# Two raw weight tiles placed in the empty half of the w_in buffer, with a new pinned order that reaches into batch 3

## The chip, the cores and the metric

The kernel runs on one core of a Trainium2 chip. The metric is the device time of one execution in microseconds (us); below, a median of three runs. The profile is one further execution recorded by the hardware profiler. PE is TensorE (matmuls), PEld its weight loads, DVE is VectorE, ACT is ScalarE, POOL is GpSimd, SP is SyncE, whose queue (SPq) issues the DMAs.

## What is computed

Slot attention over 8 batches, 8 heads, 576 positions, head size 64 and 32 slots, then a feed-forward block with weights `w_in` (512 x 2048) and `w_out` (2048 x 512):

```
a    = softmax(phi, over positions)
k_m  = einsum('bhsm,bhsd->bhmd', a, k);   v_m = einsum('bhsm,bhsd->bhmd', a, v)
attn = softmax(q @ k_m^T / 8, over slots)
x    = (attn @ v_m) with heads side by side          # 4608 x 512
out  = gelu(x @ w_in) @ w_out                        # gelu with erf
```

`w_in` and `w_out` reach the chip as 64-bit numbers, so the kernel decodes them as well.

## The kernel before

**What is on the engines.** x is never formed. For each batch `u_p` multiplies the value slots into a block of w_in (tile `pu`, line 598) and stores it as two float32r parts in a tile `U` (`Uh`, `Ul`, line 814), so that the hidden layer `h` (line 855) is attention probabilities `p_hi`, `p_lo` times U. GELU runs on ACT (`gf`, lines 867 to 876). Its result is split into `gh` (a cast) and `gl` (line 882, DVE), and `project` (line 895) multiplies these with `wo_hi` and `wo_lo` into four accumulators `acc`, 12 matmuls a step. Batches 0 and 1 go in turn over the first 8 column blocks f of the 16 of w_in, then over the last 8; batches 2 to 7 follow one after the other.

**How a weight tile is decoded.** Each f has a 1 MB raw tile, half for w_in (`Lwi`) and half for w_out (`Lwo`), loaded in two DMAs by `load_w` (line 251). For each half ACT runs `dec_b` (lines 272 and 273), DVE runs `dec_c`, `dec_g`, `dec_s` (lines 277, 281, 285) and POOL adds the two parts (`dDi`, `dDo`, line 305). The w_in half goes to `w_in_sb[:, :, f*128 : f*128+128]`; the w_out half is split into `wo_hi` (`dE`, a cast) and `wo_lo` (`dF`, line 311). `w_in_sb` has four sections of 2048 columns for each partition; columns 1024 and on of each are first written by f = 8.

**What sets the order.** `START` is a list of pieces by name and number, a letter behind a colon choosing the engine (`d` DVE, `a` ACT). It is executed as written; what is left goes by due times (`put`, `run`). At the end each engine's instructions are chained to their program order, so every engine's queue, SP's too, runs strictly in that order. `HOME` names the buffer of each tile. Raw tiles share five buffers `U0` to `U4` of 32 KB a partition with the first key and value tiles and with the U tiles.

**The start.** Batch 0's chain is `phi`, its exponential, transposes `pt` with copies to `aT` (`atc`, line 210), slot sums `pk` for keys (line 531), `km`, `tn`, copy to `k_blocks`, scores `psc` in three parts (line 615), softmax (`n_max` line 634, `n_sub` and `n_mul` line 639, `n_exp` line 646, `n_sum` line 649), transposes `pT` (line 674), `p_hi` and `p_lo` (lines 689, 693), and the first `h`. Batch 1's transposes `pt` and its `pk` follow. `W` pieces are single warm-up matmuls. `anorm` makes the reciprocal sums `rz` that `km` needs. For batch 1 the PSUM tiles of `pt`, `pk`, `tn`, `pu` and `psc` share one buffer, so each waits for the copies of the one before.

Of the kernel before, what the change touches and what calls it, by code (L numbers as in the profile page):

```python
# [35 lines left out]
o_2_0:wy1 U_3_0:U4 U_3_1:U0 o_2_1:wy1 U_3_2:U2 U_3_3:U1 kv_6_0_0:kv5 kv_6_0_1:kv3 kv_6_0_2:kv4
kv_6_0_3:kv2 kvw_6:wy1 kv_6_1_0:kv0 kv_6_1_1:kv7 kv_6_1_2:kv6 kv_6_1_3:kv1 kv_7_0_0:kv5
kv_7_0_1:kv3 kv_7_0_2:kv4 kv_7_0_3:kv2 kvw_7:wy0 kv_7_1_0:kv0 kv_7_1_1:kv7 kv_7_1_2:kv6
kv_7_1_3:kv1 o_3_0:wy1 U_4_0:U3 U_4_1:U4 o_3_1:wy1 U_4_2:U0 to_3:wy1 U_4_3:U2 o_4_0:wy1 U_5_0:U1
U_5_1:U3 U_5_2:U4 U_5_3:U0 o_4_1:wy0 o_5_0:wy1 U_6_0:U2 U_6_1:U1 U_6_2:U3 o_5_1:wy0 U_6_3:U4  # L40
to_5:wy1 o_6_0:wy0 U_7_0:U0 U_7_1:U2 U_7_2:U1 U_7_3:U3 o_6_1:wy1 o_7_0:wy0 o_7_1:wy1 to_7:wy0
# [13 lines left out]
n_sub.2 dB.2.1 dG.2.1 dC.2.1 at.1.1.0 dS.2.1 n_hi.0 at.1.0.0 Lkv.1.0.4 n_lo.0 h.0.0.0
atc.1.1.0 Lkv.1.1.0 atc.1.0.0:d at.1.0.4 n_exp.2 n_sum.2 n_inv.2 n_mul.2 atc.1.0.4:d
dB.3.1 n_hi.1 dC.3.1 dDo.2 dG.3.1 dS.3.1 dDo.3 anorm.1 at.1.1.4 n_T.2 atc.1.1.4
gelu.0.0.0 n_hi.2 Lwi.3 slots.1.0 km.1.0 Lkv.1.1.1 n_lo.2 n_lo.1 h.0.0.1 dB.3.0 dC.3.0
dS.3.0 dE.2 Up.0.2.1 Lkv.1.1.2 gelu.0.0.1 Lwo.4 Uh.0.2 Lkv.1.1.3 h.0.1.0 gelu.0.1.0
h.0.1.1 dG.3.0 dF.2 Ul.0.2 gh.0.0:a gl.0.0 dB.4.1 dC.4.1 dG.4.1 Lkv.1.1.4 slots.1.1  # L60
h.0.2.0 dS.4.1 km.1.1 slotsT.1 kT.1:d Lwi.4 dDi.3 Lwi.5 Lq.1.0 gelu.0.1.1 gh.0.1:a
dB.4.0 h.0.2.1 Up.0.3.1 p.0.0 gl.0.1 dE.3 dG.4.0 dDo.4 dE.4 dF.4 gelu.0.2.1 Uh.0.3
Ul.0.3 score.1.0 dC.4.0 dS.4.0 Lwi.6 gelu.0.2.0 h.0.3.0 Lwo.7 gh.0.2:a dF.3 dB.5.0
gelu.0.3.0 h.0.3.1 dDi.4 dB.6.0 sT.1.0.1 Lwo.5 dB.5.1 sT.1.0.0 Lwi.8 Up.0.4.1 p.0.1
dC.5.0 dS.5.0 dG.5.0 Uh.0.4:d Ul.0.4 h.0.4.0 gelu.0.3.1 gh.0.3:a max.1.0 dG.6.0 Lq.1.1
dDi.5 Up.0.5.1 h.0.4.1 sub.1.0 exp.1.0 gl.0.2 dC.6.0 gl.0.3 dG.5.1 dC.5.1 dS.5.1 sum.1.0
gelu.0.4.1 p.0.2 Uh.0.5:d Ul.0.5 inv.1.0 dDo.5 dE.5 mul.1.0 dS.6.0 score.1.1 pT.1.0
Lwo.6 dB.6.1 Lwo.8 sT.1.1.0 p.0.3 sT.1.1.1 gelu.0.4.0 Lwi.7 gh.0.4:a dF.5 dB.7.1 gl.0.4
dG.6.1 dDi.6 Up.0.6.1 Uh.0.6 ph.1.0:d dC.7.1 h.0.5.0 h.0.5.1 dB.7.0 Ul.0.6 dC.6.1
max.1.1 dG.7.0 gelu.0.5.1 gelu.0.5.0 Up.1.0.4 Uh.1.0 dC.7.0 dS.7.0 sub.1.1 h.0.6.0  # L70
gelu.0.6.0 Lphi.2.1 dDi.7 amax.2.1 gh.0.5:a Ul.1.0 gl.0.5 pl.1.0 exp.1.1 dS.6.1 dDo.6
dE.6 h.0.6.1 gelu.0.6.1 p.0.4 Up.0.7.1 Uh.0.7:d sum.1.1 dS.7.1 inv.1.1 p.0.5 gh.0.6:a
# [24 lines left out]
h.0.14.0 dG.15.1 dDo.15 h.0.14.1 gelu.0.14.0 h.0.15.0 Lq.2.0 p.0.13 dE.14 gelu.0.14.1
h.0.15.1 mr.2 Lkv.2.0.4 dF.14 gelu.0.15.0 h.1.8.0 gelu.0.15.1 gh.0.14 gl.0.14 gh.0.15:a
dE.15 anat.2 p.0.14 h.1.8.1 gelu.1.8.1 gl.0.15 Lkv.2.1.0 dF.15 p.0.15 o.0.0.15
gelu.1.8.0 gh.1.8 o.0.1.15 o.0.2.15 o.0.3.15 h.1.9.0 h.1.9.1 gelu.1.9.1 anorm.2   # L100
gelu.1.9.0 gl.1.8 Up.1.12.4 h.1.10.0 gelu.1.10.0 Lkv.2.1.1 Lkv.2.1.4 gh.1.9:a gl.1.9 Lkv.2.1.2
Lkv.3.0.0 p.1.8 p.1.9 Uh.1.12 Lkv.2.1.3 Ul.1.12 slots.2.0 slots.2.1 h.1.10.1
gelu.1.10.1 km.2.0 km.2.1 slotsT.2 h.1.11.0 kT.2:d score.2.0 gelu.1.11.0 h.1.11.1 gelu.1.11.1
sT.2.0.1 sT.2.0.0 max.2.0 gh.1.10 Lkv.3.0.1 h.1.12.0 gl.1.10 Up.2.0.4 Uh.2.0 Ul.2.0 Lphi.3.0 gh.1.11
h.1.12.1 gelu.1.12.1 gelu.1.12.0 sub.2.0 p.1.10 h.1.13.0 Lq.2.1 gh.1.12:a gl.1.11
Lphin.3 p.1.11 Lkv.3.0.2 exp.2.0 sum.2.0 gl.1.12 inv.2.0 mul.2.0 pT.2.0 score.2.1
# [1118 lines left out]
```

## Time and profile before

| | us |
|---|---|
| median of 3 runs (702.25, 702.95, 704.43) | 702.95 |
| the profiled execution, device time | 704.61 |
| its span, first to last instruction | 702.8 |
| what lies around the span | 1.81 |
| PE busy in the span | 691.1 |
| DVE, ACT, POOL busy | 388.6, 298.4, 46.6 |
| mean granted TensorE clock | 0.981 |

The clock is given as a share of 2.4 GHz, so 0.50 is the lower level, 1.2 GHz. A window row gives, for each engine, the busy us and, in brackets, how many instructions. A timeline row gives the start, the duration and the instruction; `[idle ... <-releaser]` at its end is idle time before it and what ended that. Successive short instructions overlap a little, so durations add up to somewhat more than the stretch they fill.

### The profile page before, as it was taken

What the parts mean: (1) busy time and instruction counts of PE and PEld (TensorE: products, weight loads), DVE (VectorE), ACT (ScalarE), POOL (GpSimd) and SP (SyncE); (2) the same over time, 40 slices, a digit from 0 to 9 for tenths busy, and PEclk for the clock granted to TensorE, in tenths of its full rate; (3) what the DMA queues carried; (4) which work ended last, traced back from release to release, by engine and by line L of the source; (5) the groups of instructions that cost most, each with busy time, mean ns of one, the idle gap of its engine ahead of it and who ended that gap; (6) DMA issues with size and microseconds to landing.
All of it is one profiled execution on the core that took longest, in us unless ns stands there. A gap on an engine that the chain in (4) does not pass through costs nothing.

```text
span 702.8 us, 12357 instructions
## 1 busy us (share of the span) xinstructions
PE 691.1 (98%) x4940; PEld 576.6 (82%) x4940; DVE 388.6 (55%) x705; ACT 298.4 (42%) x768; POOL 46.6 (7%) x39
## 2 busy tenths in 40 slices
...
PEclk7599999999999999999999999999999999999999
...
GB/s 318 329 211 172 154 197 62 133 29 212 86 142 117 177 217 23 65 137 159 190 1 32 82 2 31 1 98 1 30 1 31 83 1 31 1 31 0 31 1 45
DMA packets 30716, 64.37 MB, mean 92 GB/s; under 512 B 3780, under 2 KB 8644, under 8 KB 30660
## 3 DMA queue, kind: packets, MB, share of 16 engines
...
q10 hardware_dynamic: 96, 0.13, 0.1%
q14 instruction: 17, 0.14, 0.1%
...
## 4 chain that ended last, share of the span: by engine, by line
PE 94%; DMA 1%; DVE 1%; SPq 0%; ACT 0%; issue 0%
PE acc L895 50%; PE h L855 29%; PE tacc L895 6%; PE pu L598 4%; PE psc L598 1%; PE psc L506 1%; DMA raw<-w_in 1%; PE pk L531 1%; PE x L506 1%; SPq L345 0%; PE pk L506 0%; PE psc L519 0%; PE psc L560 0%; DVE aT L210 0%; PE x L519 0%
## 5 line engine op out<-in xcount | busy, mean ns | idle before, releaser
L855 PE MATMUL h<-p_hi,U 128*128 128x288 f32 x1024 | 203.8, 298 | 0.0
L895 PE MATMUL acc<-wo_hi,gh 128*128 128x512 f32 x512 | 200.6, 392 | 0.0
L895 PE MATMUL acc<-wo_hi,gl 128*128 128x512 f32 x512 | 199.7, 390 | 0.0
L895 PE MATMUL acc<-wo_lo,gh 128*128 128x512 f32 x512 | 199.6, 390 | 0.0
L867 ACT ACTIVATE gf<-h 128x256 f32<-128x256 f32 x192 | 74.0, 387 | 265.0 <-issue 206.4
L855 PEld LDWEIGHTS h<-p_hi,U 128*128 128x128 f32 x1024 | 164.0, 188 | 23.0 <-issue 8.3
L210 DVE CAST gh<-gf 128x512 fp32r<-128x512 f32 x109 | 46.9, 430 | 167.4 <-ACT gf L867 165.3
L895 PEld LDWEIGHTS acc<-wo_hi,gh 128*128 128x128 f32 x512 | 96.5, 188 | 21.1 <-DVE gl L882 3.4
L895 PEld LDWEIGHTS acc<-wo_hi,gl 128*128 128x128 f32 x512 | 96.1, 188 | 21.5 <-DVE gl L882 0.9
L895 PEld LDWEIGHTS acc<-wo_lo,gh 128*128 128x128 f32 x512 | 96.1, 188 | 15.8
L855 PE MATMUL h<-p_lo,U 128*128 128x288 f32 x512 | 108.8, 294 | 0.1
L882 DVE TENSOR_TENSOR gl<-gf,gh 128x512 fp32r<-128x512 f32 x128 | 94.3, 736 | 15.2 <-ACT gh L210 5.7
L855 PEld LDWEIGHTS h<-p_lo,U 128*128 128x128 f32 x512 | 81.4, 188 | 0.6 <-DVE p_lo L693 0.6
L814 DVE TENSOR_TENSOR U<-pu,U 128x512 fp32r<-128x512 f32 (+2 forms) x50 | 40.8, 834 | 42.0 <-ACT U L210 41.8
L869 ACT ACTIVATE tails<-h 128x32 f32<-128x32 f32 x192 | 37.4, 195 | 0.0
L598 PE MATMUL pu<-w_in_sb,kT 64*32 64x512 f32 (+2 forms) x624 | 34.4, 528 | 0.4 <-ACT kT L210 0.4
L210 ACT CAST U<-pu 128x512 fp32r<-128x512 f32 (+2 forms) x42 | 30.4, 759 | 7.4 <-PE pu L598 7.3
L305 POOL TENSOR_TENSOR w_in_sb<-y,raw 128x512 int32<-128x512 int32 x16 | 23.8, 1493 | 43.8 <-DVE y L285 11.8
L305 POOL TENSOR_TENSOR y<-y,raw 128x512 int32<-128x512 int32 x16 | 21.9, 1374 | 56.5 <-DVE y L285 23.9
L272 ACT ACTIVATE y<-raw 128x512 f32<-128x512 f32 x32 | 21.6, 675 | 8.9 <-issue 4.3
L895 PE MATMUL tacc<-wo_hi,gh_t 128*128 128x512 f32 x64 | 25.0, 391 | 0.0
L895 PE MATMUL tacc<-wo_hi,gl_t 128*128 128x512 f32 x64 | 24.9, 389 | 0.0
...
## 6 DMA issues: line engine op xcount, KB each, us to landing
...
raw<-w_out SPq DMA_DIRECT2D x16, 512.0 KB, 5.6
raw<-w_in SPq DMA_DIRECT2D x16, 512.0 KB, 4.5
out<-o SPq DMA_DIRECT2D x16, 512.0 KB, 2.7
...
aT<-phiN SPq DMA_DIRECT2D x6, 512.0 KB, 4.7
...
```

Source lines behind the costliest of these rows:

```text
L210: return e.copy(dst, src) if e is nc.scalar else e.tensor_copy(dst, src)
L272: nc.scalar.activation(y, high.bitcast(F32), AF.Abs, scale=2.0**16)
L305: nc.gpsimd.tensor_tensor(w, y, low, op=ALU.add)
L506: nc.tensor.matmul(pk[32 * j : 32 * j + 32, : 2 * D], st["aT", b][:, c, g, 32 * j : 32 * j + 32], st["kv", b, g, c][:, :, j, :], start=(c ...
L531: nc.tensor.matmul(pk[32 * j : 32 * j + 32, w0 * D : (w0 + n) * D], st["aT", b][:rows, c, g, 32 * j : 32 * j + 32], t[:rows, w0 : w0 + n, ...
L598: nc.tensor.matmul(ps[g][M * j : M * j + M], st["kT", b][rows, t, M * j : M * j + M], moving[j][rows], start=True, stop=True,)
L814: nc.vector.tensor_sub(u[:, ..., 1, :], pu, u[:, ..., 0, :].bitcast(F32))
L855: i = nc.tensor.matmul(h[:, :HS], u[g][w], x[:, g, :], start=(n == 0), stop=(n == 3 * G - 1))
L867: nc.scalar.activation(gf[:, f % 2 * n : f % 2 * n + n], h[:, :n], AF.Gelu)
L869: nc.scalar.activation(t, h[:, n:HS], AF.Gelu)
L882: nc.vector.tensor_tensor(g_of("gl", *k), g_of("gf", *k), g_of("gh", *k).bitcast(F32), op=ALU.subtract)
L895: nc.tensor.matmul(acc, x, w[:, f, :], start=(first and n == 0), stop=(last and n == 2))
```

## The change

Two raw tiles get another place: the raw tiles of f = 3 and f = 4 (`SPARE`) lie in columns 1024 and on of w_in_sb, sections 0 and 1 for f = 3, sections 2 and 3 for f = 4. `HOME` loses these two names and deals the five U buffers anew. `START` is a new list that goes on to loads, slots and scores of batches 4 to 6 and to hidden layers of batch 3. `PLACES` fixes at the start in what order tile tags get their memory. The output DMA of batches 0 and 1 is a piece of its own (`os`), so the list can put it later than the eviction. `anat` falls away, its halves `aadd` and `ax` being named apart.

```diff
 HOME = """
-raw_0:U0 ... raw_1:U2 ... raw_2:U1 ... raw_3:U0 ... raw_4:U2 ... raw_5:U3 raw_6:U1 raw_7:U0 ...
+raw_0:U0 ... raw_1:U2 ... raw_2:U1 ... raw_5:U0 raw_6:U2 raw_7:U1 ...
...
 START = """
-W.4.3 Lphi.0.0 amax.0.0 aexp.0.0 at.0.0.0 Lphi.0.1 amax.0.1 aexp.0.1 anorm.0 atc.0.0.0:d
...
+dG.1.1 atc.0.1.0 Lwi.0 dS.1.1 atc.0.0.4:a slots.0.0.0 dDo.1 Lphi.1.0 dE.1:d anorm.0 Lkv0.0.1 dF.1
...
+PLACES = """
+kT:1024*3 phi:4608*1 nm:8*2 sm:8*2 aT:5120*1 rz:8*2 ...
...
+    for x in PLACES.split():
+        tag, size, n = x.replace("*", ":").split(":")
+        sb.tile([P, int(size) // 4], F32, tag=tag, name=f"place_{tag}", bufs=int(n))
...
+    SPARE = {3: 0, 4: 2}
+
     def raw_of(f):
         def make():
-            if f == 0:
-                first_tiles()
+            if f in SPARE:
+                x = w_in_sb[:, SPARE[f] : SPARE[f] + 2, DFF // 2 :].bitcast(I32)
+                return x.rearrange("p k (n t) -> p k n t", t=2)
             return sb.tile([P, 2, DM, 2], I32, **home(f"raw_{f}"))
...
-        if f == NF - 1 and j % 2:
-            r = b * S + (j - 1) * P
...
+    def store(b, j):
+        r = b * S + (j - 1) * P
...
```

**DVE, from the maximum of the second score part of batch 0 (`mx_1`) to the product that ends its softmax (`s_1`, `smx_1`).** Tiles `y` and `raw` belong to the weight decode, `nm` to batch 1's phi. Before:

```order
L634 TENSOR_REDUCE mx_1_283<-psc_1_237 128x16
L639 TENSOR_TENSOR s_1_285<-psc_1_237,mx_1_283 128x512
L639 TENSOR_TENSOR s_0_231<-s_0_231,smx_0_249 128x512
L392 TENSOR_REDUCE nm_313<-phi_311 128x1
L649 TENSOR_REDUCE smx_1_315<-s_1_285 128x16
L653 TENSOR_SCALAR smx_1_315<-smx_1_315 128x16
L654 RECIPROCAL smx_1_315<-smx_1_315 128x16
L639 TENSOR_TENSOR s_1_285<-s_1_285,smx_1_315 128x512
```

In the changed order the last part of the same stretch, from the second sum on:

```order
L681 TENSOR_REDUCE smx_1_377<-s_1_357 128x16
L685 TENSOR_SCALAR smx_0_353<-smx_0_353 128x16
L686 RECIPROCAL smx_0_353<-smx_0_353 128x16
L313 TENSOR_SCALAR y_374<-y_374 128x512
L666 TENSOR_REDUCE mx_2_400<-psc_2_369 128x8
L671 TENSOR_TENSOR s_0_287<-s_0_287,smx_0_353 128x512
L685 TENSOR_SCALAR smx_1_377<-smx_1_377 128x16
L686 RECIPROCAL smx_1_377<-smx_1_377 128x16
L846 TENSOR_TENSOR U_0_399<-pu_0_390,U_0_399 128x2x128
L317 TENSOR_SCALAR w_in_sb<-w_in_sb 128x512
L671 TENSOR_TENSOR s_1_357<-s_1_357,smx_1_377 128x512
```

The first product (`s_0`) has moved behind the second sum, and a decode step, the third maximum, the first U and a decode step in the spare half stand ahead of the second product; the third score part on PE has moved ahead of the first `pu`.

**ACT, around the copies of batch 1's transposed phi (`aT<-pt`).** Before:

```order
L689 CAST p_hi_0_403<-pT_1_376 128x288
L210 COPY aT_396<-pt_0_397 128x4x128
L646 ACTIVATE s_2_390<-s_2_390 128x256
L272 ACTIVATE y_435<-raw_372 128x512
L273 ACTIVATE raw_372<-raw_372 128x512
L689 CAST p_hi_1_438<-pT_0_374 128x224
L689 CAST p_hi_1_438<-pT_1_376 128x224
L210 COPY aT_396<-pt_4_426 64x128
L873 ACT_TABLE_LOAD
```

And in the changed order:

```order
L721 CAST p_hi_0_443<-pT_1_410 128x288
L721 CAST p_hi_1_457<-pT_0_408 128x224
L721 CAST p_hi_1_457<-pT_1_410 128x224
L243 COPY aT_447<-pt_0_448 128x4x128 x2
L243 CAST wo_hi<-y_374 128x512
L243 COPY aT_447<-pt_4_480 64x128 x2
L721 CAST p_hi_1_457<-pT_2_489 128x64 x2
L905 ACT_TABLE_LOAD
```

All four copies are now on ACT; before, two of the four were on DVE.

**SP's queue, from the third raw tile to the loads behind batch 1's last key and value tiles (`kv_1_3`, `kv_1_4`), which wait for batch 1's first `pk`.** Before:

```order
L251 DMA raw_372<-w_in 128x1024
L345 DMA kv_1_1_483<-kv 128x512
L345 DMA kv_1_2_510<-kv 128x512
L251 DMA raw_515<-w_out 128x1024
L345 DMA kv_1_3_518<-kv 128x512
L345 DMA kv_1_4_548<-kv 64x512
L251 DMA raw_515<-w_in 128x1024
L251 DMA raw_587<-w_in 128x1024
```

And in the changed order (`w_in_sb` as a target is a raw tile in the spare half, f = 3 and then f = 4):

```order
L381 DMA kv_1_0_416<-kv 128x512
L287 DMA w_in_sb<-w_in 128x1024 x2
L357 DMA phi_486<-phiT 128x576
L381 DMA kv_1_4_518<-kv 64x512
L381 DMA kv_1_3_530<-kv 128x512
L287 DMA w_in_sb<-w_out 128x1024
L287 DMA raw_548<-w_out 128x1024
L287 DMA raw_554<-w_in 128x1024
```

The w_out half of f = 4 has moved behind the two waiting loads; the w_in halves of f = 3 and 4 and a load of batch 2's phi stand ahead of them.

## Rows read from the trace of the kernel before

**Rows 1.** The page: busy time, and granted clock in 40 slices.
```profile
PE 691.1 (98%) x4940; PEld 576.6 (82%) x4940; DVE 388.6 (55%) x705; ACT 298.4 (42%) x768; POOL 46.6 (7%) x39
...
PEclk7599999999999999999999999999999999999999
```

**Rows 2.** Windows by stage: PE, PEld, DVE, ACT, POOL busy, clock, DMA, GB/s.
```profile
15.07:25.40 10.33, 10.33 (x114) 9.38 (x114) 8.03 (x17) 3.56 (x7) 2.65 (x3) 0.50 1.03 380
...
34.00:35.74 1.74, 1.59 (x7) 0.78 (x6) 1.71 (x5) 1.73 (x4) 1.31 (x1) 0.97 0.74 298
35.74:37.51 1.77, 0.52 (x4) 0.28 (x3) 1.69 (x6) 1.07 (x5) 0.00 (x0) 1.00 0.02 9
37.51:40.90 3.39, 3.39 (x44) 2.53 (x45) 1.72 (x8) 2.63 (x6) 1.29 (x1) 0.50 0.34 117
40.90:47.33 6.43, 6.43 (x102) 5.12 (x101) 5.79 (x11) 6.25 (x16) 2.53 (x2) 1.00 1.00 358
...
60.00:120.00 60.00, 60.00 (x395) 48.62 (x394) 55.25 (x96) 42.09 (x91) 18.58 (x14) 1.00 0.37 130
120.00:360.00 240.00, 240.00 (x1876) 198.62 (x1876) 144.94 (x258) 114.67 (x271) 11.22 (x8) 1.00 0.41 124
```

**Rows 3.** Timeline of PE: start, duration, instruction, idle before.
```profile
15.07 7.06 PE L615 MATMUL psc<-k_blocks,q 128*128 128x64 f32 x32 [0.72 <-ACT k_blocks L210]
...
30.10 1.97 PE L674 MATMUL pT<-ident,s 128*128 128x128 f32 x8
31.98 1.94 PE L423 MATMUL pt<-ident,phi 128*128 128x128 f32 x8
33.57 0.76 PE L855 MATMUL h<-p_hi,U 128*128 128x288 f32 x2
...
37.51 2.52 PE L531 MATMUL pk<-kv,aT 128*32 128x128 f32 x40
...
43.59 1.43 PE L531 MATMUL pk<-kv,aT 128*32 128x128 f32 x40
...
47.33 0.50 PE L895 MATMUL acc<-wo_hi,gh 128*128 128x512 f32 x1
```

**Rows 4.** Timeline of DVE.
```profile
18.75 0.69 DVE L634 TENSOR_REDUCE mx<-psc 128x16 f32<-128x512 f32 x1 [0.67 <-PE psc L615]
...
27.66 0.69 DVE L639 TENSOR_TENSOR s<-s,smx 128x512 f32<-128x512 f32 x1
...
33.97 0.81 DVE L693 TENSOR_TENSOR p_lo<-pT,p_hi 128x288 fp32r<-128x288 f32 x2
34.70 0.68 DVE L210 COPY aT<-pt 128x512 f32<-128x512 f32 x1
...
43.81 1.10 DVE L882 TENSOR_TENSOR gl<-gf,gh 128x512 fp32r<-128x512 f32 x1 [0.29 <-ACT gh L210]
```

**Rows 5.** DVE groups by form: busy us, mean ns of one, idle before.
```profile
L281 DVE TENSOR_SCALAR raw<-raw 128x512 uint16<-128x512 uint16 x32 | 24.6, 789 | 0.1
...
L311 DVE TENSOR_TENSOR wo_lo<-y,wo_hi 128x512 fp32r<-128x512 f32 x16 | 13.2, 828 | 1.9 <-ACT wo_hi L210 1.8
```

**Rows 6.** Timeline of ACT.
```profile
34.02 0.58 ACT L210 COPY aT<-pt 128x512 f32<-128x512 f32 x1 [1.26 <-PE pt L423]
...
37.20 0.26 ACT L210 COPY aT<-pt 64x128 f32<-64x128 f32 x1 [0.69 <-PE pt L423]
```

**Rows 7.** Windows of 1 us, PE alone: busy, clock, DMA share, GB/s.
```profile
33.00:34.00 1.00, 1.00 (x7) 0.50 1.03 391
34.00:35.00 1.00, 0.85 (x4) 0.94 1.00 404
```

**Rows 8.** Timeline of SP's queue.
```profile
29.71 0.44 SPq L251 DMA_DIRECT2D raw<-w_out x1
38.23 0.90 SPq L345 DMA_DIRECT2D kv<-kv x2
```

**Rows 9.** The page's DMA issues: count, KB each, median us to landing.
```profile
raw<-w_out SPq DMA_DIRECT2D x16, 512.0 KB, 5.6
```

More of the change, by code (lines that the diff above doesn't have):

```diff
@@ L36 @@
[L36 to L41, printed above, removed]
+kv_1_0_0:kv6 y_2:wy0 U_0_0:U4 kv_1_0_1:kv1 kv_1_0_2:kv2 kv_1_0_3:kv5 kv_1_0_4:kv4 kv_1_1_0:kv3
@@ new lines @@
+kv_7_0_2:kv4 kv_7_0_3:kv2 kvw_7:wy0 kv_7_1_0:kv0 kv_7_1_1:kv7 kv_7_1_2:kv6 kv_7_1_3:kv1
+o_3_0:wy1 U_4_0:U4 U_4_1:U3 o_3_1:wy1 U_4_2:U2 to_3:wy1 U_4_3:U0 o_4_0:wy1 U_5_0:U1 U_5_1:U4
+U_5_2:U3 U_5_3:U2 o_4_1:wy0 o_5_0:wy1 U_6_0:U0 U_6_1:U1 U_6_2:U4 o_5_1:wy0 U_6_3:U3 to_5:wy1
+o_6_0:wy0 U_7_0:U2 U_7_1:U0 U_7_2:U1 U_7_3:U4 o_6_1:wy1 o_7_0:wy0 o_7_1:wy1 to_7:wy0
+"""
+PLACES = """
+kT:1024*3 phi:4608*1 nm:8*2 sm:8*2 aT:5120*1 rz:8*2 mx:72*2 smx:72*2 U0:8192*1 U4:8192*1
+kv0:2048*1 U3:8192*1 kv7:2048*1 U2:8192*1 q:4608*1 tails:8192*1 wy0:4096*1 km:1024*1
@@ L55 @@
[L55 to L72, printed above, removed]
@@ L97 @@
[L97 to L106, printed above, removed]
-h.1.13.1 gelu.1.13.0 p.1.12 ph.2.0:d Lkv.3.0.3 Lphi.3.1 h.1.14.0 sT.2.1.0 sT.2.1.1
-max.2.1 sub.2.1 gelu.1.13.1 gh.1.13 gl.1.13 h.1.14.1 exp.2.1 p.1.13 sum.2.1 pl.2.0
@@ new lines @@
+kT.1:d gelu.0.2.0 dC.4.0 Up.0.3.1 dC.4.1 dG.4.1 p.0.0 Uh.0.3 dE.3 dG.4.0 gh.0.1:a dS.4.1
+gelu.0.2.1 dS.4.0 dDo.4 Ul.0.3 dF.3 gh.0.2:a score.1.0 dDi.4 dE.4 h.0.3.0 sT.1.0.0 Lq.1.1
+dB.5.0 sT.1.0.1 Lwo.6 h.0.3.1 gl.0.1 dB.5.1 Up.0.4.1 dC.5.0 dG.5.0 p.0.1 Uh.0.4:a gelu.0.3.0
+dF.4 gelu.0.3.1 dC.5.1 dB.6.0 dS.5.0 gl.0.2 dDi.5 Ul.0.4 h.0.4.0 max.1.0 h.0.4.1 sub.1.0
+Up.0.5.1 dS.5.1 exp.1.0 dG.5.1 p.0.2 Uh.0.5:a sum.1.0 dDo.5 inv.1.0 Ul.0.5 gelu.0.4.0 dG.6.0
+Lwi.8 gelu.0.4.1 dB.6.1 Lwo.7 mul.1.0 h.0.5.0 dC.6.0 gh.0.3:a h.0.5.1 dS.6.0 dE.5 gl.0.3 dDi.6
@@ new lines @@
+score.1.1 gh.0.4:a pT.1.0 gelu.0.5.0 p.0.3 gelu.0.5.1 sT.1.1.1 amax.2.1 dC.6.1 mw.2 sT.1.1.0
+aexp.2.0 Lwo.8 gl.0.4 dG.6.1 Up.0.6.1 dF.5 p.0.4 Uh.0.6 aexp.2.1 dS.6.1 gh.0.5:d dB.7.0 dDo.6
+Ul.0.6 max.1.1 ph.1.0:a gl.0.5 Lwi.9 dB.7.1 Up.1.0.4 Lwo.9 dG.7.0 Lphin.2 dC.7.0 dE.6:a
+h.0.6.0 sub.1.1 Uh.1.0 dS.7.0 p.0.5 dC.7.1 dDi.7 exp.1.1 Ul.1.0 pl.1.0 gelu.0.6.0 dG.7.1
+Up.0.7.1 dS.7.1 h.0.6.1 Uh.0.7:a dDo.7 Ul.0.7 h.0.7.0 sum.1.1 gelu.0.6.1 inv.1.1 h.0.7.1
+gelu.0.7.0 dF.6 gh.0.6:a h.1.0.0 dE.7:a Lwi.10 gl.0.6 gelu.0.7.1 p.0.6 dF.7 dB.8.1 gh.0.7:d
@@ new lines @@
+Up.2.0.4 Lkv.3.0.0 Lq.2.1 gelu.1.12.0 h.1.13.0 os.0.1 Uh.2.0:d mw.4 h.1.13.1 gelu.1.13.0
+Lphi.5.1 Lkv.3.0.1 p.1.11 gelu.1.13.1 gh.1.12:a gl.1.12 sub.2.0 aadd.3 h.1.14.0 h.1.14.1
+gelu.1.14.0 gh.1.13:d h.1.15.0 gl.1.13 p.1.12 gelu.1.15.0 gelu.1.14.1 exp.2.0 p.1.13 gh.1.14:d
+sum.2.0 gl.1.14 inv.2.0 mul.2.0 h.1.15.1 Ul.2.0 p.1.14 gelu.1.15.1 pT.2.0 gh.1.15:a gl.1.15
+ax.3 tg.1.0 p.1.15 ph.2.0:d o.1.0.15 pl.2.0 o.1.2.15 score.2.1 h.2.0.0 sT.2.1.0 sT.2.1.1
+h.2.1.0 amax.5.0 o.1.3.15 tp.1.0 gelu.2.1.0 max.2.1 os.1.3 sub.2.1 tg.1.1 exp.2.1 Up.2.4.4
@@ new lines @@
+tg.1.2 tp.1.1 anorm.4 Uh.2.4:d o.1.1.15 os.1.1 tg.1.3 tp.1.2 Lkv.3.1.0 Lq.3.0 Ul.2.4 Lkv.3.1.3
+Lq.3.1 sum.2.1 mr.4 h.2.2.0 inv.2.1 Lkv.3.0.3 mul.2.1 Up.2.8.4 gelu.2.2.0 Lkv.3.1.2 gelu.2.0.0
+gh.2.0.0:d tp.1.3 pT.2.1 Lkv.4.1.4 gl.2.0.0 ph.2.1:a Lkv.4.0.4 h.2.3.0 Lkv.3.1.4 h.2.4.0
+gelu.2.3.0 to.1 h.2.5.0 P.2.0.0 gelu.2.5.0 gelu.2.4.0 Lkv.3.1.1 gh.2.0.1:a gl.2.0.1 Uh.2.8:d
+h.2.6.0 Ul.2.8 P.2.0.1 gelu.2.6.0 gh.2.0.2:a gl.2.0.2 h.2.7.0 P.2.0.2 gelu.2.7.0 gh.2.0.3:a
+gl.2.0.3 P.2.0.3 h.2.8.0 h.2.9.0 gelu.2.8.0 h.2.10.0 Up.2.12.4 gelu.2.10.0 gelu.2.9.0
@@ L987, in slot_attention_gelu_ffn @@
         "Lwi": lambda f: load_w(0, f), "Lwo": lambda f: load_w(1, f),
-        "Lphin": load_phin, "mw": a_out, "mr": a_back, "anat": a_nat, "aadd": a_add, "ax": a_x, "amax": a_max, "aexp": a_exp, "anorm": a_norm,
+        "Lphin": load_phin, "mw": a_out, "mr": a_back, "aadd": a_add, "ax": a_x, "amax": a_max, "aexp": a_exp, "anorm": a_norm,
         "at": a_T, "atc": a_Tc, "slots": slots, "km": slots_m,
@@ L1000, in slot_attention_gelu_ffn @@
     }
+    st.update({("far", "pu", b, f): 1 for b in range(3, B) for f in (4, 12)})
+    st.update({("far", "psc", b, 1): 1 for b in range(3, B)})
+    st.update({k: 1 for k in (("far", "xt", 3), ("far", "pu", 2, 12))})
     done = set()
@@ L1033, in prepare @@
         put(tn - 1, f"Lphin.{b}")
-        put(tn + 1, f"anat.{b}", *(f"aexp.{b}.{g}" for g in range(G)), f"anorm.{b}")
+        put(tn + 1, f"aadd.{b}", f"ax.{b}", *(f"aexp.{b}.{g}" for g in range(G)), f"anorm.{b}")
     prepare(2, T2, T2 + 5)
```

153 lines of the change are left out of this document (92 added, 61 removed).

## The prediction

> **What bounds the kernel now.** I read the page first: PE is busy for 691.1 of 702.8 us, and all of the granted clock's shortfall is in the first slices [rows 1]. The windows by stage show where the rest is. From 60 to 360 us PE is busy without a gap at the full clock, while DVE and ACT have room, DVE little of it up to 120 us (55.25 of 60) [rows 2]. So from the first `project` on, at 47.33 [rows 3], PE is the bound, and its work there is the same in both orders: the same matmuls, and by the order the same 88 changes between 32-row and full-size ones, each of which costs a fraction of a microsecond. The end of the kernel therefore moves by as much as the first `project` does, plus any wait that the new order makes later. The same six `h` and four `pu` stand ahead of it on PE in both orders, so 47.33 is a fair mark.
>
> Ahead of that mark the timeline of PE has two kinds of loss. The clock is at its lower level, 0.50, from the scores (15.07) to 34 us and again from 37.51 to 40.90 [rows 2, 7], and PE waits between 34.0 and 37.5: it is busy 1.59 of 1.74 and then 0.52 of 1.77 us [rows 2]. What it waits for there are the copies of batch 1's transposes; the last one on ACT starts at 37.20, and `pk` follows at 37.51 [rows 3, 6]. The clock falls right after that thin stretch. DVE is the engine behind most of this: from 18.75 on its timeline has no idle time up to the `p_lo` at 33.97 and the copy at 34.70 [rows 4].
>
> **The change part by part.** *Up to the first scores: nothing.* The new list no longer puts a warm-up matmul ahead of `tn`, but it puts `anorm` behind `dE.1` on DVE, and that cast waits for POOL; `km`, and with it `tn` and the scores, need `rz`. By the durations this gives about 15.0 for the first score matmul against 15.07 [rows 3]. Bounds: 0.6 earlier if `rz` is not last, 0.3 later if the weight half that the decode needs lands late. I take nothing.
>
> *DVE ahead of the transposes: later by 1.0.* In the old order 19 DVE instructions run from the first maximum at 18.75 to the product that starts at 27.66 and ends at 28.35 [rows 4]: 9.60 us, 0.505 each. The new order has 26 in that place: `dS.0.1`, `wo_lo.0`, the second maximum of batch 1's phi, `dC.2.1`, the third maximum, the first U and `dG.3.1` have come in. Seven at 0.505 are 3.5; two of them are dear, 0.79 and 0.83 [rows 5], so I take 3.6 (bounds 3.0 and 4.2). The second product then ends at 31.95. In the old order PE reached its eight `pT` transposes at 30.10, later than their data, and the next ones, `pt`, at 31.98 [rows 3]. In the new order the second half of `pT` (half of 1.97) runs from 31.95, and `pt` starts at about 32.95: 1.0 later. The first `h` comes at 34.5 instead of 33.57 [rows 3].
>
> *The copies: earlier by 1.7.* The old order needed from the start of `pt` at 31.98 to 37.51 for the copies and the small transposes [rows 3], 5.5 us, because two of four copies stood in DVE's full queue; the one at 34.70 waited for both `p_lo` [rows 4]. Now all four are on ACT, behind `p_hi`, which is done by then. `pt` 32.95 to 34.55, two copies of 0.58 [rows 6] to 35.6, the small transposes behind the first `h`, at 36.1 with the lower clock or 35.6 with the full one, 0.3 for them, two copies of 0.26 [rows 6]: `pk` starts between 36.4 and 36.9. DVE's third product, which the `pT` ahead of `pk` needs, is done at about 36.1 and could push this to 37.3. I take 36.8, 0.7 before the old 37.51; this is the net of the loss above and the gain here.
>
> *From `pk` to the mark.* The old order has no PE wait from 37.51 to 47.33 [rows 2]: 9.82 us, of which 3.39 at the lower clock. At the full clock the same work would take 9.82 - 1.70 = 8.1. So the mark comes at 36.8 + 8.1 = 44.9 if the clock stays up (2.4 earlier), or at 46.6 (0.7 earlier) if it falls for as long as before. In the new order PE is idle for about 0.5 to 1.0 us in the stretch ahead of `pk` where it idled 1.4 us, which speaks for a shorter fall or none; that it now also waits for half a microsecond ahead of the second half of `pT` speaks against it.
>
> *The two tiles in the spare half.* They let the w_in halves of f = 3 and 4 be issued ahead of the loads that wait for batch 1's `pk`; before, SP stood there from 30.15 to 38.23 [rows 8]. PE does not wait for weights in the old order, so this alone is worth nothing; what hides it is PE's own unbroken work from 37.51.
>
> *Behind the mark.* DVE is nearly full to 120 us [rows 2], so what it must do ahead of each `gl` matters. The old first `gl` ends at 44.91, 2.4 ahead of its use [rows 4]. Summing the new order by durations, the first `gl` ends near 43.1, 1.8 ahead of a mark at 44.9, and later ones keep that lead, because twelve casts `gh` go from DVE to ACT, which is busy 42 of 60 us [rows 2]. I take no new wait. The later output DMAs, `PLACES` and the split of `anat` cost nothing: PE does not wait in 120 to 360 [rows 2].
>
> **The sum.** Against the profiled execution's own 704.61: 703.9 with the clock's second fall, 702.2 without it. The median is 1.66 lower than that execution, as much as one such fall costs, so some of the timed runs may not have had it. I therefore count 0.7 and half of the 1.7, that is 1.55, against the median: **701.4**.
>
> **The rivals.** *The clock stays up from 34 us, and the fall was in the timed runs too.* Then the whole 2.4 is gained, 700.5, and 699.9 if the scores also start 0.6 earlier. For it: the shorter idle time. Against it: the 1.66 between the profiled run and the median.
>
> *The clock comes up later than before.* In the old trace it rose at 34 us, directly behind 16 transposes and with only 0.4 us of `h`: 0.50 in the window from 33, 0.94 in the next [rows 7]. In the new order the transposes are broken by DVE. If it comes up at 40.9 only, some 4.0 us from the first `h` on run at half speed, and the mark comes at 36.9 + 8.1 + 2.0 = 47.0: 0.3 gained, 702.6. The Trainium skill, TensorE: Matmul & The Clock Gate, section "Part 4: PE-mode transpose", says that transposes do not count as PE activity in the same way; by that rule the clock would wait for the `h` themselves, this rival's case. The rise behind 16 transposes speaks against it, though 0.4 us of `h` lay there too.
>
> *A weight load behind the wait on SP holds up ACT: slower.* The w_out half of f = 4 is now behind the two key and value loads that wait for `pk`, and its decode on ACT stands ahead of GELU of the third `h`, the cast of the fourth U and two `gh`; on DVE the other part of that U is behind it. Issued at about 38.5, it lands at 44.1 by the median 5.6 [rows 9]. Two ACT steps, GELU, the U cast and the DVE step take some 2.6, so U is there at 46.7; PE needs it at 44.9 + 2.8 + 0.65 = 48.35. It decides from a landing at 45.8 on; at 48 it costs 2.2 and, as PE then idles, the clock's 1.7 again: 705.3. The old order had the same load ahead of the wait, issued at 29.71 [rows 8].
>
> **How the numbers follow.** The forecast of about 701.4 has 0.40; the full gain (700.5 or less) 0.33; the late clock (702.6) 0.12; the late load or another wait of its kind in a list this long (705.3) 0.15. A measurement of this kernel can tell about 0.3%, 2.1 us, from no change: 700.84 and 705.06 are the borders. So faster 0.33, same 0.52, slower 0.15. The range goes from 699.4 (both gains, and the lower bound of the DVE stretch) to 704.6, which leaves out most of the slower case and a little below.
>
> **What would show it right or wrong.** In the changed profile: the first score matmul at 15.0; the second product of the softmax on DVE ending near 31.95 and `pt` at 32.95; `pk` between 36.4 and 37.3; the windows from 34 to 41 with a clock above the old ones; the first `project` at 45 to 46.6, and no PE idle behind it. A DVE stretch no longer than the old one, scores well ahead of 15, or a PE wait between 47 and 120 us would prove the prediction wrong.

## The result: slower by 1.2%, and the profile after

| | before | after |
|---|---|---|
| median, us (4 runs each, taken in turn) | 703.44 | 712.01 |
| lowest and highest | 702.25, 704.43 | 711.07, 712.67 |
| the profiled execution, its span | 704.61, 702.8 | 711.07, 709.3 |
| first `project` on PE in that execution (the mark) | 47.33 | 44.58 |
| device time less the mark | 657.28 | 666.49 |

The ratio is 1.0123 (95% interval 1.0105 to 1.0142). The forecast was 701.4 with a range up to 704.6, so the result lies far outside. The last line of the table splits it at once: the start came out shorter, as forecast, and 9.2 us were lost behind the mark, where the forecast took nothing.

The page of the changed kernel, the rows that answer to [rows 1]: PE has the same busy time, in a longer span.

```profile
PE 691.1 (97%) x4940; PEld 575.4 (81%) x4940; DVE 377.6 (53%) x686; ACT 306.8 (43%) x789; POOL 46.4 (7%) x39
...
PEclk8599999999999999999999999999999999999999
```

The windows by stage, in the columns of [rows 2]. The stretch from 35.74 to 40.90, where PE idled and then ran at 0.50, is now nearly full (1.48 of 1.77 and 3.28 of 3.39) and at 1.00. The stretch from 120 to 360 us, which was full, now lacks 5.85 us of PE.

```profile
35.74:37.51 1.77, 1.48 (x42) 0.97 (x41) 1.18 (x8) 1.75 (x5) 1.29 (x1) 1.00 0.42 118
37.51:40.90 3.39, 3.28 (x42) 2.72 (x42) 2.44 (x7) 3.07 (x9) 1.64 (x1) 1.00 0.79 270
...
120.00:360.00 240.00, 234.15 (x1806) 193.04 (x1812) 133.24 (x239) 113.61 (x267) 8.46 (x6) 0.99 0.40 120
```

The waits of PE from the mark to 345 us (waited for; us in total, times, longest): one wait holds most of it.

```profile
PE acc L927 <- DVE gh L243: 4.7, 1, 4.7
PE psc L538 <- DVE sT L744: 0.7, 1, 0.7
PE acc L927 <- ACT gh L243: 0.4, 1, 0.4
```

The chain of waits shows what stands ahead of it (start, us, instruction). The first four are work for batch 6's phi, of which batch 3's `project` needs nothing; `gh` and `acc` are batch 3's:

```profile
315.21 0.76 DVE nm L428
315.99 3.85 DMA row<-nm
319.90 6.34 DMA cols<-row
326.26 1.23 DVE aT L518
...
328.01 0.44 DVE gh L243
328.49 4.75 PE acc L927 x12
...
338.58 2.73 PE acc L927 x12
```

The maxima `nm` of a phi go to DRAM in one small DMA (`row`, the piece `mw`), come back spread over all partitions in a second (`cols`, `mr`), and DVE adds them (`aadd`). The timeline of DVE around it:

```profile
306.14 0.75 DVE L428 TENSOR_REDUCE nm<-phi 128x1 f32<-128x576 f32 x1
...
314.61 0.69 DVE L914 TENSOR_TENSOR gl<-gf,gh 128x512 fp32r<-128x512 f32 x1 [5.92 <-ACT gh L243]
...
326.26 1.23 DVE L518 TENSOR_TENSOR aT<-aT,cols 128x1024 f32<-128x1024 f32 x1 [7.97 <-DMA cols<-row]
...
328.01 0.43 DVE L243 CAST gh<-gf 128x512 fp32r<-128x512 f32 x1
```

The first maximum runs at 306.14. The second, `amax.6.1`, stands behind a `gl` that waits 5.92 us for ACT's cast, so it ends at 315.95. The two DMAs and the gaps around them take until 326.26. DVE stands for 7.97 us at the addition, and the cast `gh` that `project` needs is queued behind it. PE stands 4.7 us; then the clock falls. Windows of 2 us there, in the columns of [rows 2]:

```profile
324.00:326.00 2.00, 0.00 (x0) 0.00 (x0) 0.00 (x0) 0.00 (x0) 0.00 (x0) 1.00 1.04 330
...
330.00:332.00 2.00, 2.00 (x6) 1.53 (x5) 0.62 (x2) 1.32 (x5) 0.00 (x0) 0.50 0.87 338
332.00:334.00 2.00, 2.00 (x18) 1.64 (x19) 1.82 (x3) 0.00 (x0) 0.00 (x0) 0.91 0.05 17
```

With the clock at 0.50 for most of them, the twelve `acc` took 4.75 us where twelve take 2.73 at 1.00 (the chain above): 2.0 lost. Waits of 5.8 and this are 7.8 of the 9.2; the other 1.4 are no wait in the profile.

Where the distance was lost can be read in the code. The old plan put the five pieces of that round trip at steps of its own: both maxima and `mw` at 99, `mr` at 102, `aadd` at 108. The new list takes all of them but `aadd`, which keeps its step 108, and the list ends at about step 105 with `amax.6.1 mw.6 ... mr.6` among its last pieces: about three steps from request to use instead of nine.

### The profile page after: what moved, and what is told of

Same layout as the page of the kernel before. It is cut to its first block, busy times and chain, and to the rows that moved or that the text cites. A ratio compares the mean times of both kernels' runs of the same rounds, so it can differ in the third digit from the quotient of the medians.

```text
span 709.3 us, 12342 instructions
## 1 busy us (share of the span) xinstructions
PE 691.1 (97%) x4940; PEld 575.4 (81%) x4940; DVE 377.6 (53%) x686; ACT 306.8 (43%) x789; POOL 46.4 (7%) x39
## 4 chain that ended last, share of the span: by engine, by line
PE 93%; DMA 3%; ACT 1%; DVE 1%; issue 1%; POOL 0%; SPq 0%; ACTq 0%
PE acc L927 49%; PE h L887 28%; PE tacc L927 6%; PE pu L630 4%; DMA q<-qT 1%; PE psc L630 1%; PE psc L647 1%; DMA cols<-row 1%; PE psc L538 1%; PE pk L563 1%; PE x L538 1%; DMA row<-nm 1%; DMA phi<-phiT 0%; PE pt L459 0%; PE pk L538 0%
## 5 line engine op out<-in xcount | busy, mean ns | idle before, releaser
L243 DVE CAST gh<-gf 128x512 fp32r<-128x512 f32 x97 | 42.5, 438 | 172.3 <-ACT gf L899 159.7
L914 DVE TENSOR_TENSOR gl<-gf,gh 128x512 fp32r<-128x512 f32 x128 | 90.2, 706 | 46.4 <-ACT gh L243 38.7
L927 PE MATMUL tacc<-wo_lo,gh_t 128*128 128x512 f32 x64 | 24.9, 389 | 0.0
L243 ACT CAST gh<-gf 128x512 fp32r<-128x512 f32 x31 | 19.4, 626 | 11.1 <-PE acc L927 11.1
```

The costliest lines, as they stand in the source:

```text
L243: return e.copy(dst, src) if e is nc.scalar else e.tensor_copy(dst, src)
L914: nc.vector.tensor_tensor(g_of("gl", *k), g_of("gf", *k), g_of("gh", *k).bitcast(F32), op=ALU.subtract)
L927: nc.tensor.matmul(acc, x, w[:, f, :], start=(first and n == 0), stop=(last and n == 2))
```

## The experiments

Each kernel's ratio is to the old kernel on the same chip (medians of 703.3 to 703.7). Beside ratios the text uses the device time of the profiled execution less its mark, "behind the mark": it was 657.28 to 657.38 in four executions of kernels with the old order there (before, e4_tiles_only, e8_copies_on_act and e13_old_filled), so it separates what happens at the start from what happens later.

**Is it the late second maximum, and would a later addition do as well?** In the first kernel the maximum and its DMA move ahead, and the transfer back ahead of two key and value loads; in the second the addition is due two steps later.

```diff
-... amax.6.0 gl.3.0.3 ... gl.3.0.4 amax.6.1 Ul.3.12 mw.6 Lphin.6
-Lkv.6.0.1 Lkv.6.1.3 mr.6 ...
+... amax.6.0 amax.6.1 mw.6 gl.3.0.3 ... gl.3.0.4 Ul.3.12 Lphin.6 mr.6
+Lkv.6.0.1 Lkv.6.1.3 ...
```

> The second maximum of batch 6's phi and the transfer of the maxima to DRAM stand directly behind the first maximum, and the transfer back stands ahead of two kv loads; nothing else moves. Theory (a request that is issued late, and an engine that works in order): the maximum no longer stands behind a gl that waits for ACT, the round trip of 10.2 us begins some 8 us earlier, DVE's addition finds its data, PE's wait of 4.7 us at 323.8 goes and with it the clock's fall of 3.4 us at half speed behind it, 1.7: 712.0 - 6.4 = 705.6. Rival (the transfers that are bunched there make the data late whenever they are asked for): the addition still waits, 709.5 or more. Rival (another wait takes its place): PE idles elsewhere between 300 and 340, 707 to 710.

Measured 704.99, ratio 1.0023 (1.0015 to 1.0032): 7.0 less than the changed kernel. In its timeline of DVE both maxima run together, and the addition no longer waits:

```profile
306.26 1.40 DVE L428 TENSOR_REDUCE nm<-phi 128x1 f32<-128x576 f32 x2
...
317.66 1.22 DVE L518 TENSOR_TENSOR aT<-aT,cols 128x1024 f32<-128x1024 f32 x1
```

The wait of 4.7 and the fall of the clock are gone, the waits of 0.7 and 0.4 are left. The place of the second maximum, and of the transfers that follow it, is most of the result.

```diff
-    put(108, "aadd.6")
-    exps(109, 6)
+    put(110, "aadd.6")
+    exps(111, 6)
```

> Only the due time of batch 6's addition (108 to 110) and of what follows from it (109 to 111) is changed, the request stays as late as it is. Theory (what costs is the place of the addition in DVE's order, since gh and gl stand behind it): the wait and the clock's fall go as in the run with the early maximum, 705.6, with up to 1 more if slots of batch 6, due at 112, have to wait. Rival (the data themselves are what PE needs): the wait moves to slots of batch 6 and stays 4 us or more, 710 to 712.

Measured 710.58, ratio 1.0112 (1.0094 to 1.0130): only 1.4 of the loss is gone, and the interval overlaps that of the change. The time is the rival's; the wait has moved, to a place that neither side of the expectation named. Timelines of its SP queue, DVE and PE:

```profile
319.43 0.33 SPq L487 DMA_DIRECT2D cols<-row  x1
...
325.25 0.99 SPq L421 DMA_DIRECT2D q<-qT  x2
```

```profile
326.32 1.23 DVE L518 TENSOR_TENSOR aT<-aT,cols 128x1024 f32<-128x1024 f32 x1 [5.38 <-DMA cols<-row]
```

```profile
330.18 2.59 PE L630 MATMUL psc<-q,kT 64*32 64x288 f32 x32 [3.13 <-DMA q<-qT]
```

SP's queue runs in program order too. `row` stands on it until the late maximum is there (issued at 315.77, against 307.69 in e1_max_early), and what is behind it, the transfer back and then the loads of q, comes as much later: the two q transfers shown were issued at 316.89 in the old order, at 317.31 in e1_max_early, here at 325.25. PE then waits 3.13 us for q at the scores, and 3.4 us at half clock follow. So the late request has two victims: DVE's queue behind the addition, and SP's behind the two transfers. A later use mends one of them; an earlier request mends both.

**Is it the order of the transfer back on SP's queue?** Here `mr.6` moves ahead of the two key and value loads `Lkv.6.0.1 Lkv.6.1.3`, all else as in the changed kernel.

> The changed kernel with only the transfer back of batch 6's maxima put ahead of the two kv loads that stood between the two transfers; the maximum stays late. If those loads make its landing slow (6.34 us against 3.9 in the kernel before), it lands up to 2.4 earlier, PE waits 2.3 to 4 instead of 4.7, and the time is 709.5 to 711.5. If the landing is slow for the loads behind it, or for none of them, 712.0 and a landing of over 6.

Measured 711.81, ratio 1.0122 (1.0109 to 1.0135). The two DMAs took 3.64 and 5.74 us in its chain of waits, and the addition came 0.8 earlier:

```profile
325.46 1.23 DVE L518 TENSOR_TENSOR aT<-aT,cols 128x1024 f32<-128x1024 f32 x1 [7.17 <-DMA cols<-row]
```

PE's wait fell from 4.7 to 3.9, but the clock was at 0.50 for 6.8 us, 6.2 of them behind the wait, instead of 3.4. The landing and the wait came down in part, as expected if the neighbours matter, and the time did not. The neighbours of the transfer on the queue are at most a small part of the cause; e1_max_early and the next kernel show that its late start is the main one.

**Does the same lateness do it in the old order?** Old kernel, with the second maximum and `mw` at step 107 instead of 99, `mr` behind them.

```diff
-    columns(6, 96, 99, 99)
-    put(102, *heads("slots", 5), *heads("km", 5), "Lphin.6", "mr.6", *load_all(6))
+    columns(6, 96, 99, 107)
+    put(102, *heads("slots", 5), *heads("km", 5), "Lphin.6", *load_all(6))
+    put(107, "mr.6")
```

> The kernel before, with the suspected cause put in: the second maximum of batch 6's phi and its transfer to DRAM are due at 107 instead of 99, the transfer back at 107 instead of 102; the addition keeps its 108, all loads keep their places. Nothing of the changed kernel's list is in it. Theory (the distance between request and addition is what costs): the maximum comes at about 317, the data land 8 to 10 later at 325 to 328, gh and gl stand behind the addition on DVE as in the changed kernel, PE waits 3 to 6 between 322 and 330, and the clock falls behind that for 3.4 or 6.8 at half speed: 703.4 + 5 to 9, that is 708 to 712. Rival (the old order has room to take it, or the loss in the changed kernel hung on the loads that stand there): 703 to 705.

Measured 711.68, ratio 1.0109 (1.0089 to 1.0128): the result of the change, without the change. Timeline of DVE, then the wait of PE:

```profile
316.75 0.74 DVE L392 TENSOR_REDUCE nm<-phi 128x1 f32<-128x576 f32 x1
...
327.18 1.23 DVE L486 TENSOR_TENSOR aT<-aT,cols 128x1024 f32<-128x1024 f32 x1 [9.69 <-DMA cols<-row]
```

```profile
PE acc L895 <- DVE gh L210: 5.7, 1, 5.7
```

**The two small waits.** On top of e1_max_early: the slot sums of batch 4 ahead of the `sT` that PE waited for, and the cast `gh.3.0.4` on DVE instead of ACT.

```diff
-gh.2.1.0:d sT.3.0.1 slots.4.0 gl.2.1.0 slots.4.1 ...
+gh.2.1.0:d slots.4.0 slots.4.1 sT.3.0.1 gl.2.1.0 ...
-... gh.3.0.4:a gl.3.0.4 ...
+... gh.3.0.4:d gl.3.0.4 ...
```

> The run with the early maximum, and the two small waits of PE taken away as well: slots of batch 4 stand ahead of the sT of batch 3 on PE's and DVE's lists (0.73 at 250), and the cast gh.3.0.4 goes from ACT to DVE (0.41 at 314). Theory (PE is the bound everywhere else, so a wait taken away comes back in full): 704.99 - 1.14 = 703.85. Rival (PE arrives earlier at the next wait): 704.6 or more.

Measured 703.91, ratio 1.0006 (0.9994 to 1.0017): 1.1 less than e1_max_early, as expected, and not to be told from before. Its only PE wait from the mark to 345 us is one of 0.4 for an eviction.

**The two tiles alone,** in the old order: the diff's lines on `SPARE` in the old kernel, nothing else.

> The kernel before with nothing but the two raw tiles in the spare half. By the prediction they are worth nothing alone: 703.4, within 0.5. Rival (the loads of f = 3 and 4, free to land earlier, give DVE and ACT work earlier): 702.5 or less. Rival (they crowd the key and value loads of batch 1): later pk, 704.5 or more.

Measured 703.38, ratio 1.0000 (0.9989 to 1.0010). The tiles are worth nothing by themselves. This profile of the old order has earlier times than [rows 3]; its timeline of PE, and that of the kernel before ahead of its scores:

```profile
13.32 7.06 PE L620 MATMUL psc<-k_blocks,q 128*128 128x64 f32 x32 [1.00 <-ACT k_blocks L210]
...
35.90 2.52 PE L536 MATMUL pk<-kv,aT 128*32 128x128 f32 x40
...
45.70 0.50 PE L900 MATMUL acc<-wo_hi,gh 128*128 128x512 f32 x1
```

```profile
9.83 0.78 PE L531 MATMUL pk<-kv,aT 128*32 128x64 f32 x32 [2.43 <-DMA kv<-kv]
```

The same list starts its scores at 13.32 here and at 15.07 in [rows 3]; there the first `pk` had waited 2.43 us for its keys, here 1.41. The execution on which the prediction rests was a late one of its kind.

**The list cut short.** If the end of the list is the fault, the plan could do the rest. Cut behind `p.1.15`, early in batch 2:

> The pinned list ends behind the last project of batch 1, where the old one ended; the rest goes by the plan, as before. Theory (the list's first part gives 2.7, its new part costs everything else): no PE wait behind the first project, 703.4 - 2.7 = 700.7. Rival (the gain of the start is given back between the first project and the end of batch 1 by more or dearer changes between matmul forms): 702.5 to 703.5. Rival (the plan's due times don't fit the new first part either): a PE wait between 190 and 340, 704 or more.

Measured 712.77, ratio 1.0136 (1.0121 to 1.0151): my expectation was wrong, and the seam had only moved, as its second rival had it. Timelines of DVE and PE, then a window of 4 us within the wait:

```profile
202.96 2.48 DVE L962 TENSOR_TENSOR o<-acc,part 128x512 f32<-128x512 f32 x4
```

```profile
203.70 0.80 PE L898 MATMUL tacc<-wo_hi,gh_t 128*128 128x512 f32 x1 [8.30 <-DVE o L962]
```

```profile
198.00:202.00 4.00, 0.00 (x0) 0.00 (x0) 2.73 (x5) 1.06 (x2) 0.00 (x0) 0.61 0.00 0
```

Where the plan takes over, its overdue pieces, batch 2's softmax, come ahead of batch 1's evictions on DVE, and PE waits 8.3 us for these. The clock falls within the wait, at 198.9, and is at 0.50 for 10.2 us, 5.4 of them behind the wait. Cut behind `to.1` instead, where batch 1 is evicted:

> The pinned list ends behind batch 1's tail (to.1), six lines further than in the run with the short list; the rest goes by the plan. In that run everything of batch 2 that was overdue came ahead of batch 1's evictions on DVE, and PE waited 8.3 for its bank. Theory (a list may end where no overdue work stands ahead of what PE waits for; behind it the plan's due times keep the distance that the old kernel had): no PE wait behind the first project, the start's 2.7 is kept of which up to 1.7 was clock that many runs of before had anyway: 700.9 to 702.0. Rival (the plan's order has a wait behind any list that isn't its own): a PE wait of over 1 between 200 and 340, 704 or more.

Measured 702.99, ratio 0.9997 (0.9989 to 1.0006). From the mark on PE waits once, 0.3 us. The first `project` is at 44.73, and 657.76 lie behind it. I had expected 700.9 to 702.0, so the gain is smaller: the new start alone does not gain 0.2%.

**The copies on ACT alone.** In the old list the two copies of batch 1's phi that DVE makes go to ACT (`atc.1.0.0:a`, `atc.1.0.4:a`), which was my reason for the earlier `pk`.

> The kernel before with only the two copies of batch 1's transposes that stood on DVE moved to ACT. By the prediction's term for the copies pk starts up to 1.7 earlier, since DVE's stretch ahead of it is not lengthened here, and the clock may stay up: 703.63 - 1.0 to - 2.5, that is 701.1 to 702.6. Rival (ACT is as late as DVE there, with the cast of p_hi ahead): pk within 0.3 of the old one, 703.3 to 704.

Measured 704.30, ratio 1.0014 (1.0002 to 1.0026). The timeline of PE, and a window behind it:

```profile
35.92 2.50 PE L531 MATMUL pk<-kv,aT 128*32 128x128 f32 x37 [0.46 <-ACT aT L210]
...
47.00 0.50 PE L895 MATMUL acc<-wo_hi,gh 128*128 128x512 f32 x1
```

```profile
38.00:40.00 2.00, 2.00 (x14) 1.46 (x6) 1.25 (x6) 1.45 (x4) 0.00 (x0) 0.50 0.82 227
```

`pk` starts at 35.92, against 35.90 in e4_tiles_only, as the rival had it. The last copy now waits in ACT's queue as long as it did in DVE's, and PE's stretch ahead of `pk` is broken otherwise, with the clock at 0.50 behind it. In the old list, which engine makes the copies is not the lever.

**Can the start be used further?** In the profiles of the changed kernel and of e7_list_to_tail PE runs at half clock from about 11.5 to 35.5 us. Further `W` pieces, warm-up matmuls that compute nothing, fill its gaps from 4 to 30 us: sixteen on the kernel of e7_list_to_tail and on that of e6_three_mends, and fourteen, in like places, on the old one (the expectations' fifteen in all and twelve are miscounts).

```diff
-... aexp.0.0 at.0.1.4 ... slots.0.0.0 ... slots.0.1.0 km.0.1.0 slotsT.0.0 ... n_score.0 ...
-... slotsT.0.1 ... W.3.29 kT.0.1 ... Up.0.0.1 ... n_T.0 ...
+... aexp.0.0 W.4.0 W.4.1 W.4.2 at.0.1.4 ... W.4.14 W.4.15 slots.0.0.0 ...
+... W.4.16 W.4.17 W.4.18 slots.0.1.0 km.0.1.0 W.4.19 slotsT.0.0 ... W.3.20 W.3.21 n_score.0 ...
+... W.3.25 slotsT.0.1 ... W.3.26 W.3.27 W.3.28 W.3.29 Up.0.0.1 ... W.3.30 n_T.0 ...
```

> The run with the list up to the tail, and warm-up matmuls on PE ahead of the steps that wait between 4.7 and 29 us, fifteen in all where there were three, into banks that nothing uses then; their results are not read. Theory (the clock falls at 11 to 13 because PE idles 8 of the first 14 us, and a PE that is kept busy keeps it up or gets it back earlier): a granted clock above 0.50 in some of the stretch from 13 to 34, the first project up to 4 earlier, 699 to 702. Rival (the start is bound by loads and DVE, or the clock falls whatever PE does there): the first project within 0.5 of 44.7 and 702.5 to 703.5; later by up to 0.5 where a filler stands in the way.

Measured 701.58, ratio 0.9970 (0.9960 to 0.9980): faster than both kernels, and 1.4 less than e7_list_to_tail (1.9 by the two ratios, since these ran on different chips). Windows from 12 and from 28 us, in the columns of [rows 2], of e7_list_to_tail and then of this kernel:

```profile
12.00:20.00 8.00, 6.84 (x38) 6.34 (x34) 3.59 (x7) 4.41 (x9) 0.69 (x1) 0.50 1.03 398
...
28.00:36.00 8.00, 7.29 (x58) 5.32 (x56) 7.50 (x21) 6.53 (x18) 1.29 (x1) 0.53 0.79 282
```

```profile
12.00:20.00 8.00, 5.05 (x56) 4.34 (x44) 4.67 (x11) 3.65 (x9) 1.33 (x1) 1.00 1.03 383
...
28.00:36.00 8.00, 6.99 (x67) 5.00 (x66) 7.39 (x21) 7.22 (x19) 1.80 (x2) 0.86 0.93 331
```

The clock stays at 1.00 until 19.9 us and is back at 30.1. This profile is of the slowest of ten executions (703.31), in which the scores waited 1.65 us for q and a `pk` 1.50 us for keys; its first `project` comes at 45.42, later than the 44.73 of e7_list_to_tail, so it shows the higher clock and not the gain.

> The run with the three mends (the whole new list, without its late maximum and its two small waits) and the same fillers at the start as in the filled run. Theory (the clock at the start is worth about 1.4 to a kernel whose PE never waits behind it, whatever list follows): 703.9 - 1.4 = 702.5. Rival (the gain of the filled run came from elsewhere): 703.9.

Measured 702.15, ratio 0.9984 (0.9975 to 0.9993): 1.8 less than without the fillers (1.5 by the ratios). In the two profiles the first `project` is 0.5 earlier, at 44.20 against 44.66; that the clock gives the rest is argued, not shown.

> The kernel before with twelve more warm-up matmuls ahead of the steps at which its PE waits up to 27 us; nothing of the new list. Theory (the fillers alone keep the clock up for part of the start, the old list gains as much as the new one): 703.6 - 1.4 or more, 701.0 to 702.3, with a granted clock above 0.50 in some of the stretch from 13 to 30. Rival (only the new list's start can use a faster PE there, since DVE is what the old one waits for from 18.75 on): 703 to 704.

Measured 702.91, ratio 0.9998 (0.9989 to 1.0008). No gain clear of the noise, close to the rival's 703 to 704: its timeline of PE shows waits for DVE, the longest of them below, and in the window from 34 us the clock is at 0.50 again.

```profile
30.06 1.06 PE L423 MATMUL pt<-ident,phi 128*128 128x128 f32 x8 [1.21 <-DVE U L814]
```

```profile
34.00:36.00 2.00, 1.28 (x13) 0.72 (x15) 1.94 (x6) 0.59 (x2) 0.00 (x0) 0.50 0.04 14
```

## Why the prediction was wrong

**The step that failed** is "Behind the mark": "I take no new wait." It looked at `gl` and at how full DVE is up to 120 us, and for all of 120 to 360 us it concluded from the old trace's full PE that nothing could cost anything. But that row showed the old plan's distances, and the new list had taken over just these pieces. The order of the changed kernel showed the second maximum close ahead of its addition, three steps or about 6.5 us (in the old trace two steps take 4.3 us: twelve `acc` begin at 306.85, 311.16 and 315.45). The old trace shows 3.23 us between the issues of the two DMAs for batch 7 (328.93 and 332.16) and one landing of `cols`, 3.9 us, together 7.1. That sum was to be had, and I made it only for the start; it would have shown that there was no slack, not the size of the loss, since the trip took 10.2 us and began late behind the `gl`. My signs of being wrong named a PE wait between 47 and 120 us; it came at 323.8. Four experiments bear on it: the early maximum removes 7.0 of 8.6 us, the old order with a late maximum shows the same loss, and moving the use or the neighbours of the transfer does not mend it. With the two small waits another 1.1 goes, which leaves 703.91, not to be told from before. Behind the mark 1.4 us more than before are left there, of which 0.4 are a wait. The traces place most of it early: batch 1's tail (the first `tacc`) begins 151.4 to 151.5 us behind the mark in before, e4_tiles_only and e13_old_filled, and 152.6 to 152.7 in the changed kernel, e1_max_early, e6_three_mends and e7_list_to_tail, with PE busy all the way. Why stays open.

**The rival for slower was of the right kind in the wrong place.** "Or another wait of its kind in a list this long" had 0.15 together with the late weight load. That load did not strike: in the timeline of ACT of the changed kernel its decode waited 0.40 us, at 43.45, ahead of the 45.8 from which it would have decided.

```profile
43.45 0.68 ACT L308 ACTIVATE y<-w_in_sb 128x512 f32<-128x512 f32 x1 [0.40 <-DMA w_in_sb<-w_out]
```

The price of 3.9 that I gave such a wait was too small as well.

**The start, step by step.** In the changed kernel's timeline of PE and DVE:

```profile
13.75 7.06 PE L647 MATMUL psc<-k_blocks,q 128*128 128x64 f32 x32 [0.72 <-issue]
...
31.92 1.97 PE L459 MATMUL pt<-ident,phi 128*128 128x128 f32 x8
...
36.15 1.43 PE L563 MATMUL pk<-kv,aT 128*32 128x128 f32 x40 [0.29 <-ACT aT L243]
...
44.58 0.50 PE L927 MATMUL acc<-wo_hi,gh 128*128 128x512 f32 x1
```

```profile
17.43 0.69 DVE L666 TENSOR_REDUCE mx<-psc 128x16 f32<-128x512 f32 x1 [1.74 <-PE psc L647]
...
22.10 1.73 DVE L347 TENSOR_TENSOR wo_lo<-y,wo_hi 128x512 fp32r<-128x512 f32 x1 [0.25 <-ACT wo_hi L243]
...
29.94 0.71 DVE L671 TENSOR_TENSOR s<-s,smx 128x512 f32<-128x512 f32 x1
```

- *Scores at 15.0:* 13.75, by my own signs a mark against the prediction. Both lists can do this (13.32 in e4_tiles_only); 15.07 was the old kernel's late keys in one execution.
- *DVE's stretch of 13.2 us from the first maximum to the end of the second product:* 17.43 to 30.65 is 13.2. That this is right to a tenth is luck: the seven new instructions at the prices that I named are 4.1 and not 3.6 (five at 0.505, 0.79 and 0.83), and `wo_lo` took 1.73 us and not 0.83, with 0.25 of idle ahead of it; the rest of the stretch was shorter by as much. `pt` came 1.3 after the product (31.92), not 1.0.
- *`pk` 3.85 after `pt`:* 4.2, and the clock stays at 1.00 from there on, as the rival "the clock stays up" had it. The clock rose at about 35.4, behind the transposes and the first `h`, a little later than in [rows 7]. The Trainium skill, TensorE: Matmul & The Clock Gate, section "Part 4: PE-mode transpose", says that transposes do not count as PE activity in the same way; two other runs do not agree with that. In e4_tiles_only, below, a mean of 0.58 in the window from 30 us and 1.00 behind it put the rise at 31.7, ahead of the first `h`, and from 28.4 on PE had run nothing but sixteen transposes; in e9_back_first, with the new start, the clock rose at 33.5 and the first `h` began at 33.87.

```profile
30.24 1.75 PE L428 MATMUL pt<-ident,phi 128*128 128x128 f32 x8
31.75 0.51 PE L860 MATMUL h<-p_hi,U 128*128 128x288 f32 x2
```

```profile
30.00:32.00 2.00, 2.00 (x12) 1.79 (x10) 1.86 (x6) 1.01 (x3) 0.74 (x1) 0.58 1.06 420
```

- *From `pk` to the mark 8.1 at the full clock:* 8.4 (36.15 to 44.58). With `pt` and `pk` above, the start is 1.0 longer than my sum with the clock up, so that from the scores to the mark it gains 1.4 (30.83 against 32.26) and not 2.4.
- *My reason for it, the copies on ACT,* is not borne out: alone in the old list they gain nothing.
- *The mark 0.7 to 2.4 earlier:* 2.75 between the two profiled executions, but the old one was late. With what lies behind the mark taken as fixed for a list, medians give its usual place: 703.4 - 657.3 = 46.1 for the old start, 702.99 - 657.76 = 45.2 for the new one in e7_list_to_tail and 712.01 - 666.49 = 45.5 in the changed kernel. So the start gains about 0.6 to 0.9 (an estimate from these rows) where I counted 1.55. Setting a term from one execution against the median was the mis-sized part. I took the 1.66 between that execution and the median for a fall of the clock that some runs lack. But e4_tiles_only, at 703.05, has the fall too (its `pk` takes 2.52 us, as in [rows 3]), and so have e8_copies_on_act, e10_old_late_max and e13_old_filled (2.52, 2.51, 2.52); what it lacks is the late keys.
- *The two tiles, nothing:* right, 1.0000.
